# Value products of a pair of heads in two groups instead of five, in an attention and two-FFN kernel

## The chip, the cores and the metric

The kernel runs on one NeuronCore of a Trainium2 chip. The metric is device time in microseconds of one execution of the whole program, the median over several runs. Engines are named as in the profile: PE is TensorE (its weight loads, PEld, overlap its matmuls), DVE is VectorE, ACT is ScalarE, POOL is GpSimd, SP is SyncE.

## The reference

```
# q, k, v: (4 batches, 8 heads, 576 rows, 64 columns), float32; tau = 0.02
scores = matmul(q, k^T) / sqrt(64)
scores = where(scores >= max(scores) - tau, scores, -1e9)
attn   = exp(scores - max(scores));  attn = attn / (sum(attn) + 1e-9)
x      = matmul(attn, v), heads side by side      # 2304 tokens x 512
h      = x @ w_in;  g = max(h, 0) + alpha * min(h, 0);  x = g @ w_out       # 512 -> 2048 -> 512
h      = x @ w_in2; g = h * clip(h + 3, 0, 6) / 6;      out = g @ w_out2
```

## The kernel before

The work is cut into 16 pairs of heads (4 batches of 4 pairs) and into FFN passes. A pair has two heads with 576 query rows each. They are handled in nine score tiles (`NT = 9`): tiles 0 to 7 are four blocks of 128 queries, first head and second head in turn, and tile 8 holds the last 64 queries of both heads at once. Two tiles make a unit, the odd tile t of each couple ends it, and tile 8 is a unit of its own. So a pair has five units, which end at t = 1, 3, 5, 7 and 8, and cover 128, 128, 128, 128 and 64 queries of both heads.

For each tile, `do_S` forms the scores on PE (float32r) in PSUM, and `soft` takes the row maximum (DVE), the exponential (ACT) and the threshold with the row sum (DVE). At the end of a unit, `soft_norm` divides on POOL and DVE, `do_T` transposes the probabilities on PE, 128 columns at a time, and copies each bank of four transposes from PSUM to the tile `p` in SBUF with ACT (L427 for four blocks, L430 for the remaining one). `do_PV` then multiplies by the values.

A value product is an accumulation over five blocks of keys, for two heads. A value block is the 128x64 stationary operand, and the transposed probabilities of the unit are the moving operand: 128 queries, or 64 in the last unit. The first head writes partitions 0 to 63 of a PSUM tile of the pool `ps_ho`, the second head partitions 64 to 127. The operands are plain float32, and each such matmul appears in the trace as two load-and-multiply couples, so a group of one unit is 2 x 5 x 2 = 20 matmul rows on L444. ACT copies the group's result into `xo` (L450). After the last unit the pair's `xo` goes out: in the first batch it is split for the FFN's input, in later batches it is written to DRAM by two DMAs of SP.

`ps_ho` has two buffers. They are used in turn by the first FFN product `h` (L216, 12 matmuls of 512 columns), the second FFN product `o` (L245 in the first layer, L251 in the second, 12 matmuls of 512 columns for a tile), the value products `pv`, and, for the first pairs, transposes of inputs (L322). An `h` tile is read by ACT (`m`, L221 or L229) and then DVE (`g`, L223 or L231) before its buffer comes free; an `o` tile by ACT or DVE into `acc` (L504, L506, L508).

The attention of batch 0 runs first. From then on the FFN passes of the batch before are spread over the attention of the next one: after each score tile the main loop issues a proportional share of the FFN queue. Attention work is issued with a raised priority, and a planner orders the instructions of each engine before the program is built, by its own estimate of times. Within the first pass over each weight, weights that arrive as 64-bit numbers are decoded by ACT, DVE and POOL (L148 to L154) and written to a scratch in DRAM. The last FFN passes (the last batch, and all the 64-row remainders) run alone after the attention is over.

Of the kernel before, what the change touches and what calls it, by code (L numbers as in the profile page):

```python
# [9 lines left out]
F32 = mybir.dt.float32  # L10
# [9 lines left out]
P = 128  # L20
# [7 lines left out]
def f32(ap):  # L28
    return ap.bitcast(F32)
# [3 lines left out]
def kernel(  # L33
# [13 lines left out]
    nc = tc.nc  # L47
    B, H, S, D = q.shape
# [4 lines left out]
    SM = 512  # L53
    SR = S - SM
    SH = S // 2
    NP = H // 2
    NT = 9
    PB = NP * NT
    NB = S // P
# [11 lines left out]
    rem_blk = B  # L71

    dram = ctx.enter_context(tc.tile_pool(name="dram", bufs=1, space=DRAM))
    x1d = [dram.tile([ND, P, n], F32, name=f"x1d{i}") for i, n in enumerate(blocks)]

    def pool(stack, name, bufs, **kw):
        return stack.enter_context(tc.tile_pool(name=name, bufs=bufs, **kw))
# [22 lines left out]
    def split(hi, lo, src, lo_eng):  # L100
        nc.scalar.copy(hi, src)  # L101
        lo_eng.tensor_tensor(out=lo, in0=src, in1=f32(hi), op=ALU.subtract)  # L102
# [22 lines left out]
    for i in range(3 if wide else 0):  # L125
        t = const.tile([P, RA * RB, 2], U32, name=f"raw64{i}")
# [59 lines left out]
    def fetch(kind, c):  # L186
        if c < len(passes) * NF and (kind, c) not in ws:
            nm, ft, _, _, fresh = w_of(kind, c)
            w_fetch((kind, c), nm, ft, fresh)
# [71 lines left out]
    a3 = pool(att, "a3", 3, side="right")  # L261
    ps_s = pool(psum, "ps_s", 2, space=PSUM)
    ps_t = pool(psum, "ps_t", 2, space=PSUM)
    ps_ho = pool(psum, "ps_ho", 2, space=PSUM)
# [3 lines left out]
    for i in range(2):  # L268
        t = a1.tile([P, 2, P], F32R, tag=f"qr{i}", name=f"qr{i}")
# [5 lines left out]
    for i in range(2):  # L275
        t = a1.tile([P, 2, NB + 1, D], F32, tag=f"v{i}", name=f"v{i}")
# [9 lines left out]
    st = {}  # L286
# [61 lines left out]
    def prep(pi, t):  # L348
        if pi >= len(pairs):
            return  # L350
        if t == 0:
            prep_split(pi, "k")
        if t == 2:
            prep_load(pi, "v")
        if t in (1, 2, 3):
            prep_t(pi, "k", t - 1)
        if t == 3:
            prep_split(pi, "q")
            prep_load(pi + 1, "k")
        if t in (4, 5, 6):  # L360
            prep_t(pi, "q", t - 4)
        if t == 6:
            prep_load(pi + 1, "q")


    def do_S(i):
        pi, t = divmod(i, NT)
        s = st[pi]
        ps = ps_s.tile([P, 2, 512], F32, tag="s", name="s")
        if TILES[t] is None:  # L370
            mms = [(qr[pi % 2][:, h, :], h * W, a) for h in range(2) for a in range(2)]
        else:
            h, j = TILES[t]
            mms = [(s["q"][:, h * W + j * P:h * W + j * P + P], h * S, a) for a in range(2)]
        for half in range(2):
            for n, (w, c, a) in enumerate(mms):
                nc.tensor.matmul(ps[:, half, 0:SH], lhsT=w, rhs=s["k"][:, a, c + half * SH:c + half * SH + SH],  # L377
                                 start=(n == 0), stop=(n == len(mms) - 1))
        st[i, "s"] = ps
# [9 lines left out]
    def soft(i):  # L389
        h = 0 if TILES[i % NT] is None else TILES[i % NT][0]  # L390
        if h == 0:
            e = a3.tile([P, 2 * S], F32, tag="e", name="e", bufs=4)
            st["e"] = e, small("sm", 2, 3)
        e, sm = st["e"]
        ps = st.pop((i, "s"))[:, :, 0:SH]
        eh = v2(e[:, h * S:h * S + S])
        nmx, thr = small("nmx"), small("thr")
        nc.vector.tensor_reduce(out=nmx, in_=ps, axis=AX.XY, op=ALU.max, negate=True)  # L398
        nc.scalar.activation(eh, ps, AF.Exp, bias=nmx, scale=1.0)  # L399
        nc.vector.tensor_scalar(out=thr, in0=nmx, scalar1=-1.0, scalar2=ntau_sb, op0=ALU.mult, op1=ALU.add)  # L400
        nc.vector.scalar_tensor_tensor(out=eh, in0=ps, scalar=thr, in1=eh, op0=ALU.is_ge, op1=ALU.mult, accum_out=sm[:, h:h + 1])  # L401

    def soft_norm(n, tile_i):
        e, sm = st["e"]
        den, rc = small("den", 2), small("rc", 2, 3)
        nc.gpsimd.tensor_scalar(out=den[:, 0:n], in0=sm[:, 0:n], scalar1=1.0, scalar2=1e-9, op0=ALU.mult, op1=ALU.add)
        if wide and tile_i in EARLY:
            raw = raws[EARLY[tile_i]]
            nc.gpsimd.tensor_scalar(out=f32(raw[:, DM, :]), in0=den, scalar1=0.0, scalar2=0.0, op0=ALU.mult, op1=ALU.mult)
        nc.vector.reciprocal(rc[:, 0:n], den[:, 0:n])  # L410
        for h in range(n):
            eh = e[:, h * S:h * S + S]
            nc.gpsimd.tensor_scalar(out=eh, in0=eh, scalar1=rc[:, h:h + 1], scalar2=0.0, op0=ALU.mult, op1=ALU.add)  # L413
        if n == 1:
            nc.gpsimd.tensor_scalar(out=e[:, S:W], in0=e[:, SM:S], scalar1=1.0, scalar2=0.0, op0=ALU.mult, op1=ALU.add)

    def do_T(n):
        e, _ = st["e"]  # L420
        pt = a3.tile([P, 2 * NB + 1, P], F32, tag="p", name="p")
        for h in range(n):
            ps = ps_t.tile([P, NB, P], F32, tag="t", name="t")
            for kt in range(NB):
                c = h * W + kt * P
                nc.tensor.transpose(ps[:, kt], e[:, c:c + P], ident)  # L426
            nc.scalar.copy(pt[:, h * NB:h * NB + NB], ps)  # L427
        ps = ps_t.tile([P, SM], F32, tag="t", name="r")[:, 0:P]
        nc.tensor.transpose(ps, e[:, SM:W], ident)  # L429
        nc.scalar.copy(pt[:, 2 * NB], ps)  # L430
        return pt


    def do_PV(i, n, pt):
        pi, t = divmod(i, NT)
        b, hp = pairs[pi]
        vn = vs[pi % 2]
        m = P if n == 2 else SR
        pv = ps_ho.tile([P, SM], F32, tag="ho", name="pv")[:, 0:m]
        for kt in range(NB + 1):  # L440
            for h in range(2):
                blk = 2 * NB if kt == NB else kt + NB * h * (n - 1)
                c = SR * h * (2 - n)
                nc.tensor.matmul(pv[64 * h:64 * h + 64, :], lhsT=vn[:, h, kt, :], rhs=pt[:, blk, c:c + m],  # L444
                                 start=(kt == 0), stop=(kt == NB), skip_group_check=True)
        if "xo" not in st[pi]:
            st[pi]["xo"] = a2.tile([P, S], F32, tag="xo", name="xo")
        xo = st[pi]["xo"]
        j = t // 2
        nc.scalar.copy(xo[:, j * P:j * P + m], pv)  # L450
        if n == 1:
            if b == 0:
                split(x0[:, 0, hp], x0[:, 1, hp], xo[:, 0:SM], nc.gpsimd)
            else:
                nc.sync.dma_start(x1d[b][hp], xo[:, 0:SM])
            nc.sync.dma_start(x1d[rem_blk][hp, :, b * SR:(b + 1) * SR], xo[:, SM:S])
            del st[pi]

    box = {}
# [63 lines left out]
    def new_x():  # L526
        return xp.tile([P, 2, NKT, SM], F32R, tag="x", name="x")
# [16 lines left out]
    x0 = new_x()  # L544
# [25 lines left out]
    for i in range(NS):  # L570
        pi, t = divmod(i, NT)
        with tc.high_priority(offset=50):
            prep(pi + 1, t)
            do_S(i)
            soft(i)
        if t % 2 == 1 or t == NT - 1:
            with tc.high_priority(offset=50):
                n = 1 + t % 2
                soft_norm(n, i)
                do_PV(i, n, do_T(n))  # L580
            if i in EARLY:
                if len(ws) < 7:
                    ready(*EARLY[i])
                at = early.index(EARLY[i]) + 2
                if at < len(early):
                    fetch(*early[at])
        if i % PB == PB - 1:
            emitted.add(i // PB)
        while done < min(len(queue), (i + 1 - PB - LAG) * per):
            f, a = queue[done]  # L590
            f(*a)
            done += 1
# [16 lines left out]
    for layer in (1, 2):  # L609
# [6 lines left out]
        for m in range(len(seq) + LAGO):  # L616
            if m < len(seq):
                ft, blk = seq[m]
                n = blocks[blk]
                h = ps_h.tile([P, SM], F32, tag="h", name="h")  # L620
# [10 lines left out]
            ft, blk = seq[m - LAGO]  # L631
            gs = gss.pop(m - LAGO)
            n = blocks[blk]
# [3 lines left out]
            if layer == 1:  # L637
                for d in range(ND):
                    o = oa[d][:, 0:n] if blk < B else orr[d // 2][:, (d % 2) * 256:(d % 2) * 256 + n]
# [3 lines left out]
            else:  # L643
                for d in range((n + P - 1) // P):
                    o = oa[d] if blk < B else orr[d]
                    mm_o2(o, ws["o", c0 + ft], gs, d, n, first_, last_)
                    if last_:
                        t = ob.tile([P, SM], F32, tag="ob", name="ob")
# [38 lines left out]
```

## Time and profile before

| | |
|---|---|
| median of three runs | 1163.09 us (1161.37, 1163.09, 1163.73) |
| the profiled execution, its own time | 1161.51 us |
| its span in the profile | 1159.7 us |
| busy: PE, PEld, DVE, ACT, POOL | 1117.4, 927.7, 606.1, 697.6, 674.9 us |
| matmul rows, of them on L444 | 6944, of them 1600 |

The span is the time from the first to the last instruction of the profiled execution; 1.8 us of its own time lie around it. Busy times overlap across engines. A matmul's duration in the trace includes its passage through the array, so that consecutive matmuls overlap, and the distance from start to start tells more than the duration.

### The profile page before, as it was taken

To read this page: it belongs to the slowest core of one execution; us is meant where nothing else is said; L and a number is where in the kernel's file an instruction comes from. 1 tells how busy PE (TensorE), PEld (TensorE's weight loads), DVE (VectorE), ACT (ScalarE), POOL (GpSimd) and SP (SyncE) were. 2 spreads that over 40 slices of the span, in tenths; PEclk is the share of its full clock that TensorE was granted. 3 is DMA by queue.
4 is the path that set the end of the run, shared out by engine and by line. 5 is a ranking of instruction groups with operands and counts; after the bars stand their busy time and mean duration, and the time that the engine had idled before them with its cause. 6 is when DMAs were issued, how large, how long until landed. Compare 5 with 4: busy or idle time off the path is not lost.

```text
span 1159.7 us, 19517 instructions
## 1 busy us (share of the span) xinstructions
PE 1117.4 (96%) x6944; PEld 927.7 (80%) x6944; DVE 606.1 (52%) x1215; ACT 697.6 (60%) x1352; POOL 674.9 (58%) x726
## 2 busy tenths in 40 slices
PE   6998999999899999999999999999999999999998
PEld 5776888877778878787888888787878888888886
DVE  6889779898796616373454526273325222232221
ACT  6988888888877656465656555465435333344332
POOL 3777789998887755545456756544444343334432
PEclk9999999999999999999999999999999999999999
DMA  5546347765765432333324431322236222222211
GB/s 164 158 129 199 108 152 229 237 213 177 247 190 170 147 100 81 114 92 95 107 64 144 134 110 55 103 68 73 73 90 184 64 64 64 64 64 57 63 37 55
DMA packets 92770, 137.51 MB, mean 119 GB/s; under 512 B 19328, under 2 KB 48512, under 8 KB 92672
## 3 DMA queue, kind: packets, MB, share of 16 engines
q1 hardware_dynamic: 92672, 136.26, 39.7%
q8 instruction: 55, 0.90, 0.3%
q14 instruction: 43, 0.35, 0.1%
HBM read 101.72 MB, written 25.17 MB: 109 GB/s over the span
## 4 chain that ended last, share of the span: by engine, by line
PE 82%; ACT 7%; DVE 3%; DMA 3%; issue 2%; POOL 1%; SPq 0%; ACTq 0%; DVEq 0%; POOLq 0%
PE h L216 31%; PE o L245 14%; PE o L251 13%; PE s L377 6%; PE pv L444 6%; PE t L426 4%; PE r L251 2%; PE r L245 2%; PE pt L322 2%; ACT low L148 1%; ACT e L399 1%; ACT f L149 1%; PE r L429 1%; DMA wo<-f 1%; ACT p L427 1%
## 5 line engine op out<-in xcount | busy, mean ns | idle before, releaser
L216 PE MATMUL h<-x,wi 128*128 128x512 f32 (+1 forms) x1536 | 355.4, 380 | 1.4 <-DVE g L231 1.0
L216 PEld LDWEIGHTS h<-x,wi 128*128 128x128 f32 x1536 | 272.3, 188 | 54.3 <-ACT wi L101 1.2
L241 POOL TENSOR_TENSOR gs<-g,gs 128x512 fp32r<-128x512 f32 (+1 forms) x160 | 191.1, 1194 | 199.2 <-ACT gs L237 198.8
L251 PE MATMUL o<-wo,gs 128*128 128x512 f32 x768 | 194.1, 397 | 6.4 <-DVE g L231 4.2
L245 PE MATMUL o<-gs,wo 128*128 128x512 f32 x768 | 194.9, 397 | 3.7 <-DVE acc L506 1.4
L251 PEld LDWEIGHTS o<-wo,gs 128*128 128x128 f32 x768 | 140.2, 188 | 39.6 <-DVE g L231 6.5
L245 PEld LDWEIGHTS o<-gs,wo 128*128 128x128 f32 x768 | 140.2, 188 | 34.3 <-DVE acc L506 2.0
L223 DVE SCALAR_TENSOR_TENSOR g<-m,rest_sb,h 128x512 f32<-128x512 f32 x80 | 55.4, 693 | 174.8 <-ACT m L221 172.2
L231 DVE SCALAR_TENSOR_TENSOR g<-m,h 128x512 f32<-128x512 f32 x80 | 50.6, 632 | 164.4 <-ACT m L229 164.2
L102 POOL TENSOR_TENSOR wi<-st,wi 128x512 fp32r<-128x512 f32 x56 | 72.2, 1289 | 98.3 <-ACT wi L101 97.8
L401 DVE SCALAR_TENSOR_TENSOR e<-s,thr,e 128x576 f32<-128x576 f32 x144 | 116.0, 813 | 20.3 <-ACT e L399 17.8
L413 POOL TENSOR_SCALAR e<-e,rc 128x576 f32<-128x576 f32 x144 | 107.2, 755 | 26.7 <-DVE rc L410 22.5
L398 DVE TENSOR_REDUCE nmx<-s 128x1 f32<-128x576 f32 x144 | 107.6, 752 | 27.6 <-PE s L377 26.8
L229 ACT ACTIVATE m<-h,three 128x512 f32<-128x512 f32 x80 | 51.5, 645 | 116.5 <-PE h L216 116.5
L237 ACT CAST gs<-g 128x512 fp32r<-128x512 f32 (+1 forms) x160 | 93.2, 582 | 46.4 <-DVE g L231 15.1
L399 ACT ACTIVATE e<-s,nmx 128x576 f32<-128x576 f32 x144 | 106.8, 748 | 23.3 <-DVE nmx L398 22.1
L221 ACT ACTIVATE m<-h 128x512 f32<-128x512 f32 x80 | 44.5, 556 | 104.9 <-PE h L216 104.8
L444 PE MATMUL pv<-p,v 128*64 128x128 f32 (+1 forms) x1600 | 105.3, 268 | 1.9 <-ACT p L427 1.1
L377 PE MATMUL s<-ka,qt 128*128 128x288 f32 x512 | 100.8, 320 | 6.2 <-DVE thr L400 3.9
L444 PEld LDWEIGHTS pv<-p,v 128*64 128x64 f32 x1600 | 82.4, 137 | 23.0 <-issue 16.4
L102 POOL TENSOR_TENSOR wo<-st,wo 128x512 fp32r<-128x512 f32 x56 | 74.3, 1342 | 43.9 <-ACT wo L101 43.9
L101 ACT CAST wo<-st 128x512 fp32r<-128x512 f32 x96 | 57.1, 619 | 60.2 <-DMA st<-wo 52.0
(88 smaller groups left out, 1625.5 us busy)
## 6 DMA issues: line engine op xcount, KB each, us to landing
st<-wi SPq DMA_DIRECT2D x96, 256.0 KB, 2.6
st<-wo SPq DMA_DIRECT2D x96, 256.0 KB, 2.7
raw<-in_moe_w_in_dram SPq DMA_DIRECT2D x32, 512.0 KB, 4.3
raw<-in_moe_w_out_dram SPq DMA_DIRECT2D x32, 512.0 KB, 4.2
ka<-ka SPq DMA_DIRECT2D x30, 304.0 KB, 4.1
wi<-f SPq DMA_DIRECT2D x32, 256.0 KB, 4.0
wo<-f SPq DMA_DIRECT2D x32, 256.0 KB, 3.7
raw<-in_k_dram SPq DMA_DIRECT2D x16, 256.0 KB, 3.4
```

Of the source, the lines that this page charges most:

```text
L102: lo_eng.tensor_tensor(out=lo, in0=src, in1=f32(hi), op=ALU.subtract)
L216: nc.tensor.matmul(h[:, :n], lhsT=w[:, ws, kt * P:(kt + 1) * P], rhs=x[:, xs, kt, :n], start=(i == 0), stop=(i == len(steps) - 1))
L237: nc.scalar.copy(gs[:, 0, :n], g[:, :n])
L241: nc.gpsimd.tensor_tensor(out=gs[:, 1, :n], in0=g[:, :n], in1=f32(gs[:, 0, :n]), op=ALU.subtract)
L245: nc.tensor.matmul(o[:, :n], lhsT=w[:, ws, dt * P:(dt + 1) * P], rhs=gs[:, gsel, :n], start=fresh and start and i == 0, stop=stop and i == ...
L251: nc.tensor.matmul(o[:m, :], lhsT=gs[:, gsel, tt * P:tt * P + m], rhs=w[:, ws, :], start=start and i == 0, stop=stop and i == 2)
L377: nc.tensor.matmul(ps[:, half, 0:SH], lhsT=w, rhs=s["k"][:, a, c + half * SH:c + half * SH + SH], start=(n == 0), stop=(n == len(mms) - 1))
L398: nc.vector.tensor_reduce(out=nmx, in_=ps, axis=AX.XY, op=ALU.max, negate=True)
L399: nc.scalar.activation(eh, ps, AF.Exp, bias=nmx, scale=1.0)
L401: nc.vector.scalar_tensor_tensor(out=eh, in0=ps, scalar=thr, in1=eh, op0=ALU.is_ge, op1=ALU.mult, accum_out=sm[:, h:h + 1])
L413: nc.gpsimd.tensor_scalar(out=eh, in0=eh, scalar1=rc[:, h:h + 1], scalar2=0.0, op0=ALU.mult, op1=ALU.add)
L444: nc.tensor.matmul(pv[64 * h:64 * h + 64, :], lhsT=vn[:, h, kt, :], rhs=pt[:, blk, c:c + m], start=(kt == 0), stop=(kt == NB), skip_group_ ...
```

## The change

From the second batch on, nothing is multiplied at the ends of units t = 1 and t = 5. At t = 3 one group takes the units of t = 1 and t = 3 together, with 256 queries as one moving operand of two runs of 128. At t = 8 one group takes the units of t = 5 and t = 7 in the same way (256 queries), then the last unit's 64 queries into the columns behind them, so that one PSUM tile holds 320 columns. ACT's copy into `xo` follows the group: 256 and 320 columns in place of four of 128 and one of 64. In the first batch the value products stay five groups.

The tile `p` becomes two tiles that hold two units each (`p`, two buffers), and one for the last unit (`p1`, one buffer), in place of three tiles of one unit. The transposes and their copies write the same blocks into the new places.

```
-    def do_T(n):
+    def do_T(n, t):
         e, _ = st["e"]
-        pt = a3.tile([P, 2 * NB + 1, P], F32, tag="p", name="p")
+        if n == 1:
+            pt = a3.tile([P, 1, NB + 1, P], F32, tag="p1", name="p1", bufs=1)
+        elif t % 4 == 1:
+            pt = a3.tile([P, 2, 2 * NB + 1, P], F32, tag="p", name="p", bufs=2)
+        else:
+            pt = st["p"][0]
+        dst = pt[:, t % 4 // 2 if n == 2 else 0]
...
-            nc.scalar.copy(pt[:, h * NB:h * NB + NB], ps)
+            nc.scalar.copy(dst[:, h * NB:h * NB + NB], ps)
...
-        nc.scalar.copy(pt[:, 2 * NB], ps)
-        return pt
+        nc.scalar.copy(dst[:, n * NB], ps)
+        st["p"] = st.get("p", []) * (t % 4 != 1) + [pt] * (n == 1 or t % 4 == 1)

-    def do_PV(i, n, pt):
+    def do_PV(i):
...
-        m = P if n == 2 else SR
-        pv = ps_ho.tile([P, SM], F32, tag="ho", name="pv")[:, 0:m]
-        for kt in range(NB + 1):
-            for h in range(2):
-                blk = 2 * NB if kt == NB else kt + NB * h * (n - 1)
-                c = SR * h * (2 - n)
-                nc.tensor.matmul(pv[64 * h:64 * h + 64, :], lhsT=vn[:, h, kt, :], rhs=pt[:, blk, c:c + m],
-                                 start=(kt == 0), stop=(kt == NB), skip_group_check=True)
+        if b == 0:
+            parts = [(1, st["p"][1], 0)] if t == NT - 1 else [(2, st["p"][0], t % 4 // 2)]
+        elif t in (3, NT - 1):
+            parts = [(2, st["p"][0], None)] + [(1, p1, 0) for p1 in st["p"][1:]]
+        else:
+            return
+        pv = ps_ho.tile([P, SM], F32, tag="ho", name="pv")
+        at = 0
+        for n, pt, u in parts:
+            m = SR if n == 1 else P if u is not None else 2 * P
+            for kt in range(NB + 1):
+                for h in range(2):
+                    blk = n * NB if kt == NB else kt + NB * h * (n - 1)
+                    o = pv[64 * h:64 * h + 64, at:at + m]
+                    if n == 1:
+                        r = pt[:, 0, blk, SR * h:SR * h + m]
+                    elif u is None:
+                        o, r = o.rearrange("p (u q) -> p u q", u=2), pt[:, :, blk, :]
+                    else:
+                        r = pt[:, u, blk, :]
+                    nc.tensor.matmul(o, lhsT=vn[:, h, kt, :], rhs=r, start=(kt == 0 and at == 0), stop=(kt == NB), skip_group_check=True)
+            at += m
...
-        j = t // 2
-        nc.scalar.copy(xo[:, j * P:j * P + m], pv)
-        if n == 1:
...
+        end = S if t == NT - 1 else t // 2 * P + P
+        nc.scalar.copy(xo[:, end - at:end], pv[:, 0:at])
+        if t < NT - 1:
+            return
...
                 soft_norm(n, i)
-                do_PV(i, n, do_T(n))
+                do_T(n, t)
+                do_PV(i)
```

## Rows read from the trace of the kernel before

**Rows 1.** The page: PE's line of busy times, and the granted clock in 40 slices.
```profile
PE 1117.4 (96%) x6944; PEld 927.7 (80%) x6944; DVE 606.1 (52%) x1215; ACT 697.6 (60%) x1352; POOL 674.9 (58%) x726
...
PEclk9999999999999999999999999999999999999999
```
**Rows 2.** Three stretches: from:to, length, busy time by engine, clock, DMA.
```profile
117.00:200.00 83.00, 82.66 (x549) 69.47 (x549) 65.18 (x135) 69.20 (x135) 67.95 (x75) 1.00 0.55 167
200.00:350.00 150.00, 140.83 (x867) 114.69 (x866) 129.49 (x250) 124.75 (x231) 130.24 (x131) 1.00 0.68 209
350.00:865.00 515.00, 507.30 (x3156) 417.12 (x3155) 240.61 (x473) 291.97 (x569) 285.55 (x296) 1.00 0.35 102
```
**Rows 3.** The chain that ended last, same stretches in the same order, shares by line.
```profile
by line: PE h L216 34.0%; PE o L245 26.7%; PE s L377 13.1%; PE pv L444 10.5%; PE t L426 9.3%; PE pt L322 4.0%; PE r L429 1.4%; ACT e L399 0.8%; ACT p L427 0.6%; PE pt L325 0.4%; issue 0.1%
...
by line: PE h L216 17.6%; PE o L245 7.8%; PE o L251 6.9%; issue 6.4%; DMA wo<-f 5.3%; ACT f L149 4.8%; ACT low L148 4.2%; PE s L377 4.2%; DMA wi<-f 3.8%; ACT e L399 3.1%; ACT gs L237 2.4%; PE pv L444 2.1%; DMA raw<-in_moe_w_out_dram 2.1%; A
...
by line: PE h L216 34.1%; PE o L251 17.8%; PE o L245 17.6%; PE s L377 7.2%; PE pv L444 7.2%; PE t L426 5.9%; PE pt L322 1.6%; issue 1.6%; PE r L429 1.0%; ACT m L229 0.8%; ACT wi L101 0.7%; DVE g L231 0.7%; DMA st<-wo 0.5%; DVE acc L508 0.4%
```
**Rows 4.** The tile pv alone, same stretches: busy PE, PEld, ACT, with counts.
```profile
117.00:200.00 83.00, 9.69 (x140) 7.37 (x140) 1.90 (x7) 1.00 0.55 167
200.00:350.00 150.00, 13.42 (x220) 10.97 (x220) 2.84 (x11) 1.00 0.68 209
350.00:865.00 515.00, 50.53 (x840) 41.32 (x840) 10.55 (x42) 1.00 0.35 102
```
**Rows 5.** The timeline of PE around two value groups: start, length, what.
```profile
424.08 1.31 PE L444 MATMUL pv<-p,v 128*64 128x128 f32 x20
425.33 3.01 PE L245 MATMUL o<-gs,wo 128*128 128x512 f32 x12
428.27 0.80 PE L444 MATMUL pv<-p,v 128*64 128x64 f32 x20
429.00 0.33 PE L429 MATMUL r<-ident,e 128*128 128x128 f32 x1
```
**Rows 6.** The timeline of PE cut to one couple before each group's edge.
```profile
427.95 0.39 PE L245 MATMUL o<-gs,wo 128*128 128x512 f32 x1
...
425.12 0.28 PE L444 MATMUL pv<-p,v 128*64 128x128 f32 x2
```
**Rows 7.** Groups by line and shape: count, busy us, mean ns, idle before.
```profile
L444 PE MATMUL pv<-p,v 128*64 128x128 f32 x1280 | 91.5, 279 | 0.8 <-DVE g L231 0.8
...
L444 PEld LDWEIGHTS pv<-p,v 128*64 128x64 f32 x1600 | 82.4, 137 | 23.0 <-issue 16.4 <-ACT p L427 1.4 <-DVE g L231 1.0
L427 ACT COPY p<-t 128x512 f32<-128x512 f32 x144 | 82.3, 596 | 11.6 <-PE t L426 11.5
...
L450 ACT COPY xo<-pv 128x128 f32<-128x128 f32 x64 | 17.1, 267 | 6.8 <-PE pv L444 6.2
...
L444 PE MATMUL pv<-p,v 128*64 128x64 f32 x320 | 13.8, 227 | 1.1 <-ACT p L427 1.1
...
L450 ACT COPY xo<-pv 128x64 f32<-128x64 f32 x16 | 3.5, 216 | 15.7 <-PE pv L444 15.6
```
**Rows 8.** PE's waits from 350 to 865: in total, times, longest.
```profile
PE o L251 <- DVE g L231: 2.2, 6, 0.4
...
PE o L245 <- DVE g L223: 0.6, 2, 0.3
```
**Rows 9.** The timeline around one such wait, PE and DVE.
```profile
408.83 1.31 PE L444 MATMUL pv<-p,v 128*64 128x128 f32 x20
410.43 0.50 PE L245 MATMUL o<-gs,wo 128*128 128x512 f32 x1 [0.29 <-DVE g L223]
...
409.63 0.75 DVE L223 SCALAR_TENSOR_TENSOR g<-m,rest_sb,h 128x512 f32<-128x512 f32 x1 [1.72 <-ACT m L221]
```
**Rows 10.** PE's waits from 200 to 350: in total, times, longest.
```profile
PE o L251 <- DVE g L231: 2.0, 3, 1.2
...
PE o L245 <- ACT xo L450: 1.4, 1, 1.4
```

More of the change, by code (lines that the diff above doesn't have):

```diff
@@ L448, in do_PV @@
         xo = st[pi]["xo"]
-        j = t // 2
-        nc.scalar.copy(xo[:, j * P:j * P + m], pv)
-        if n == 1:
[L452 to L457, printed above, removed]
+        end = S if t == NT - 1 else t // 2 * P + P
+        nc.scalar.copy(xo[:, end - at:end], pv[:, 0:at])
+        if t < NT - 1:
+            return
+        if b == 0:
+            split(x0[:, 0, hp], x0[:, 1, hp], xo[:, 0:SM], nc.gpsimd)
+        else:
+            nc.sync.dma_start(x1d[b][hp], xo[:, 0:SM])
+        nc.sync.dma_start(x1d[rem_blk][hp, :, b * SR:(b + 1) * SR], xo[:, SM:S])
+        del st[pi]
     box = {}
```

## The prediction

> **What bounds the kernel now.** I read the page first. PE is busy 96% of the span, no other engine above 60%, and its granted clock is full in every slice [rows 1], the 2.4 GHz level, so the clock plays no part. An average of that kind hides stages, so I next cut out the time in which batches 1 to 3 do their attention, 117 to 865 us, in three stretches [rows 2]. From 117 to 200 PE is busy all but 0.3 us, from 350 to 865 all but 7.7 of 515. In between, from 200 to 350, PE lacks 9.2 us of 150 and DVE, ACT and POOL are each busy 125 to 130: there the weights are decoded beside the attention. The chain of waits says the same [rows 3]: in the first and third stretch nearly all of it is PE's lines, and L444 holds 10.5% and 7.2%. In the middle one the PE lines add up to about 39%, the rest passes between ACT, DMA and issue. After 865 no value product runs. So an instant of PE saved from 117 to 200 or from 350 to 865 shortens the program, and one saved from 200 to 350 only in part.
>
> The value products of the twelve changed pairs are 140 + 220 + 840 = 1200 rows on L444 [rows 4], 100 to a pair: 1.4 pairs in the first stretch, 2.2 in the second, 8.4 in the third.
>
> **What a group costs on PE.** A group of 128 queries has 20 rows. They last 1.31 us together and one lasts 0.279 [rows 5, 7], so starts are (1.31 - 0.279) / 19 = 0.054 us apart. The two heads run side by side on the two halves of the array, so I count couples: 0.109 us each, ten of them 1.09. For 64 queries it is (0.80 - 0.227) / 19 = 0.030, a couple 0.060, ten 0.60.
>
> A group costs more than its couples. From its first start to the next group's start are 1.25 us, and 0.73 for 64 queries [rows 5]. On the way in, the 512-column matmul ahead of the group starts 0.32 us before it [rows 6, 5], where such matmuls otherwise stand (3.01 - 0.39) / 11 = 0.24 apart [rows 5, 6]: 0.08 more. On the way out, the last couple starts 0.21 us ahead of the next group where couples stand 0.109 apart. So a group of 128 costs 1.25 + 0.08 = 1.33 us, of which 0.24 are its edges; one of 64 costs 0.81, of which 0.21 are edges.
>
> **The change, part by part.** *Wider matmuls.* No row has a plain float32 moving operand of 256 columns. If it costs what two of 128 do, a couple takes 0.218 us; the straight line through 0.060 and 0.109 gives 0.207. I take 0.216, near the upper end, since 128 columns are the nearer row, and keep both. Ten couples are 2.16 (2.07 to 2.18) and a group 2.40 with its edges.
>
> *Fewer groups.* A pair costs 4 x 1.33 + 0.81 = 6.13 us before. After, it costs 2.40 at t = 3 and 2.40 + 0.60 = 3.00 at t = 8, where the 64 queries follow with no edge between: 5.40. That saves 0.73 a pair, nearly all of it edges of the three groups that go (0.69). In the two PE-bound stretches it is 9.8 x 0.73 = 7.2 us. In the middle, 2.2 x 0.73 = 1.6 are saved on PE, and I take the 39% that PE holds of the chain: 0.6 (0 to 1.6).
>
> *Waits behind short groups.* `h`, `o` and `pv` share two PSUM buffers, so behind `h` and `pv` an `o` needs the buffer of that `h`. At 408.83 a value group begins after `h`; DVE reads that `h` until 410.38 and `o` starts at 410.43, after a wait of 0.29 [rows 9]. The reader needs 1.55 us from the end of `h`, longer than a group of 1.33 and shorter than one of 2.40. Where no value group stands any more, `o` takes the other buffer. Either way the wait goes. From 350 to 865 there are 2.2 + 0.6 = 2.8 us of it, eight times [rows 8]. I take all (0 to 2.8). From 200 to 350 waits of the kind are 2.0 and 1.4 us [rows 10]; I take none (0 to 3.4), as other engines set the pace there.
>
> *ACT's copies.* Before, 4 x 267 + 216 = 1284 ns a pair. No row copies 256 or 320 columns; between 267 ns for 128 and 596 for 512 [rows 7] a line gives 377 and 431, so 0.48 us less a pair, 5.7 in all. ACT is busy 292 of 515 us in the long stretch, and PE's work hides the copies; I count nothing. In the middle stretch 2.2 x 0.48 = 1.0 us at most.
>
> *New waits.* The group at t = 3 waits for the same copies of `p` as the unit of t = 3 did. At t = 8 the 64-query part waits for the last unit's copies on L427 (and a 128-column one, which a copy of that size on L450 puts at 0.27): 0.6 + 0.27 us, hidden under the 2.16 of the 256-query part ahead of it in PE's queue. Without that cover it would be 0.9 a pair. The products of t = 1 and t = 5 are later by two and three score tiles; nobody reads `xo` before t = 8, and the DMAs of SP are issued there as before, with the same bytes.
>
> *The tiles.* The transposes and their copies are as many and as large. A `p` tile is written again six or more tiles after its last reader: with twelve pairs in 748 us [rows 2] a tile is 6.9 us, so the cover is over 40 us, and the cost nothing. The first batch keeps its five groups and its order.
>
> *The sum.* 7.2 + 0.6 + 2.8 = 10.6 us. The profiled execution took 1161.5, so 1150.9; the median of the runs lies 1.6 above it, which gives 1152.5, and I write 1152. Bounds of the costs: at the small end, edges in the PE-bound stretches alone and couples of 0.218, 9.8 x 0.69 = 6.8; at the large end 12 x 0.73, the flat line (12 x 20 x 0.009 = 2.2), both kinds of waits (2.8 + 3.4) and ACT's 1.0: 18.2. That is 1145 to 1156.
>
> **A page against the rows.** A couple of 128 stands 0.109 us apart, and one of 64, with stationary operands of the same size (all 1600 loads are 128x64 [rows 7]), 0.060. So the loads are not what sets 0.109, and wider operands buy no cheaper columns. The Trainium skill, TensorE: Matmul & The Clock Gate, Part 2, step 3, says that throughput is purely one column a cycle, which would make 128 columns 0.053 us at 2.4 GHz and leave about half of 0.109 to something else that merging halves. The trace does not agree with that for these float32 operands, as the 0.049 us between the two rows for 64 further columns shows.
>
> **Rivals.** *The loads were the bound after all.* Then a couple of 256 would cost 0.109 and each of the two merged groups in a pair save another 1.07 us: 12 x 2.14 = 26 more, 1127. The 0.060 couple speaks against it.
>
> *The edges go, but half of the gain comes back.* The planner orders all queues anew, and a PE with fewer edges meets other waits: the same stretch has waits of PE on DVE and ACT that now last tenths. Half of 10.6 leaves 1158. For it speaks that PE has 7.7 us idle in 515 already; against it, that FFN work fills PE at any time and the others are half idle.
>
> *No change.* The pace is set elsewhere, say by the share of FFN work that the main loop lets out for each score tile. Then fewer edges become idle time: 1162 to 1164. The long stretch, with PE at 98.5%, speaks against it.
>
> *Slower: the long group holds up the softmax.* PE works in order, so a score matmul or transposes queued behind a merged group come 2.40 - 1.33 = 1.07 us later at t = 3 and 3.00 - 0.81 = 2.19 at t = 8: 3.26 a pair, 39 us over twelve. Where the attention's chain is the path, that is lost. It is partly so from 200 to 350, where ACT's exponential and the scores stand in the chain [rows 3]: 2.2 x 3.26 = 7.2 there. The break-even is 10.6 of 39, 27%; at 40%, 15.6 - 10.6 = 5 us slower, 1168. Against it: the earlier units' groups no longer stand in that queue, and other engines have over 200 us to spare in the long stretch.
>
> **Numbers.** The forecast 0.62, loads 0.03, half of it 0.13, no change 0.10, slower 0.12. What a measurement of this kernel can tell from no change is about 0.2%, 2.3 us. So faster 0.78, same 0.10, slower 0.12. The range goes from 1146, near the large end, up over the case of half the gain to 1162: it leaves out the loads, the slower case and some of no change, about 0.2. The forecast's own range is 1146 to 1157.
>
> **What would show it.** L444 should have 400 + 720 = 1120 rows, in batches 1 to 3 with 480 of 256 columns and 240 of 64; twenty of 256 should last about 0.108 x 19 + 0.35 = 2.4 us. The stretch that was 350 to 865 should be shorter by some 9 us, the first by 1, the middle by 1 or less, and the time up to 117 and after 865 unchanged. The waits of `o` on DVE `g` should be gone there. I am wrong if a couple of 256 columns differs much from 0.216, if the long stretch has as much more idle PE as it has fewer edges, or if the middle grows.

## The result and the profile after

The changed kernel takes 1145.32 us (median, 1144.27 to 1146.52), the kernel before 1163.09. The ratio is 0.985, with a 95% interval from 0.984 to 0.987: 17.3 us faster. The forecast was 1152, 10.6 us faster, and 1145.3 lies just under its range. The prediction's sum had its large end at 18.2 us, 1145; the range that it wrote began at 1146. So the direction was right and the gain some 60% larger than forecast.

The profiled execution after took 1145.86 us, with a span of 1144.1; that is 15.7 us less than the profiled one of before, and the accounts below are of these two. It is less than 17.3 because the profiled execution of before was 1.6 us faster than its median. The page after, PE's line and the granted clock:

```profile
PE 1109.8 (97%) x6464; PEld 913.9 (80%) x6464; DVE 611.9 (53%) x1215; ACT 692.4 (61%) x1316; POOL 681.5 (60%) x726
...
PEclk9999999999999999999999999999999999999999
```

Against [rows 1], PE is busy 7.6 us less, and the rest of the span, in which PE does nothing, fell from 42.3 to 34.3, by 8.0. The forecast had 7.8 us of work (8.8 saved on PE, of which it let 7.8 count) and 2.8 of waits. So the work came out nearly as foretold, and the idle time fell by almost three times as much.

The value products after, by line and shape:

```profile
L464 PE MATMUL pv<-p,v 128*64 128x256 f32 x480 | 57.7, 384 | 0.3 <-DVE acc L525 0.3
...
L464 PE MATMUL pv<-p,v 128*64 128x128 f32 x320 | 28.1, 285 | 0.0
...
L464 PE MATMUL pv<-p,v 128*64 128x64 f32 x320 | 13.2, 223 | 1.1 <-ACT p L433 1.1
...
L470 ACT COPY xo<-pv 128x320 f32<-128x320 f32 x12 | 5.3, 439 | 5.3 <-PE pv L464 5.3
...
L470 ACT COPY xo<-pv 128x256 f32<-128x256 f32 x12 | 4.4, 368 | 3.8 <-PE pv L464 3.8
```

The counts are as foretold, 480 + 240 rows in batches 1 to 3. ACT's copies cost 439 and 368 ns, where a line through two rows gave 431 and 377. PE's timeline around one group at t = 8:

```profile
422.30 0.95 PE L377 MATMUL s<-ka,qt 128*128 128x288 f32 x6
423.18 2.96 PE L464 MATMUL pv<-p,v 128*64 128x256 f32 x40
426.07 3.02 PE L245 MATMUL o<-gs,wo 128*128 128x512 f32 x12
```

All 40 rows, 256 and then 64 columns, stand in one piece. From its first start to the start of `o` are 2.89 us. With 0.09 for the way in that is 2.98, where the forecast had 3.00. So the price of a group was right, that of the wider operand with it.

Where the time went is seen by cutting both traces at the same work: the starts of the 1st, 385th and 1153rd matmul row on L216. Windows before (from:to, length, busy PE, PEld, DVE, ACT, POOL, clock, DMA):

```profile
122.60:394.90 272.30, 262.74 (x1656) 216.47 (x1654) 218.79 (x429) 218.06 (x411) 228.37 (x233) 1.00 0.63 193
394.90:872.60 477.70, 470.40 (x2903) 386.89 (x2902) 215.94 (x425) 267.62 (x522) 255.91 (x265) 1.00 0.33 95
```

The same after:

```profile
122.50:392.70 270.20, 264.36 (x1518) 215.15 (x1517) 225.04 (x439) 220.71 (x403) 232.10 (x240) 0.99 0.63 196
392.70:857.10 464.40, 460.67 (x2581) 373.96 (x2580) 215.56 (x414) 259.81 (x494) 259.92 (x261) 1.00 0.34 97
```

Ahead of and behind these windows the two kernels differ by 0.1 us each. The first of the two is 2.1 us shorter, the second 13.3. But the first also holds more work: without value products (418 rows of it before, 258 after) it has 1260 rows where it had 1238. These 22 rows of scores and transposes last about 0.12 us each from start to start, an estimate of 2.7 us. At equal work the first window gains 4.8 us and the second 10.6; the forecast had 2.1 and 8.4 for them. PE's idle time falls from 9.6 to 5.8 in the first and from 7.3 to 3.7 in the second.

### The profile page after: what moved, and what is told of

Same layout as the page of the kernel before. It is cut to its first block, busy times and chain, and to the rows that moved or that the text cites. A ratio compares the mean times of both kernels' runs of the same rounds, so it can differ in the third digit from the quotient of the medians.

```text
span 1144.1 us, 18508 instructions
## 1 busy us (share of the span) xinstructions
PE 1109.8 (97%) x6464; PEld 913.9 (80%) x6464; DVE 611.9 (53%) x1215; ACT 692.4 (61%) x1316; POOL 681.5 (60%) x726
## 4 chain that ended last, share of the span: by engine, by line
PE 81%; DVE 5%; ACT 4%; issue 4%; POOL 3%; DMA 2%; SPq 0%; DVEq 0%; ACTq 0%; POOLq 0%
PE h L216 32%; PE o L245 14%; PE o L251 13%; PE pv L464 7%; PE s L377 6%; PE t L432 4%; PE r L251 2%; PE r L245 2%; PE pt L322 1%; DVE nmx L398 1%; DVE e L401 1%; DMA st<-wo 1%; POOL nat L102 1%; DVE low L150 1%; POOL gs L241 1%
## 5 line engine op out<-in xcount | busy, mean ns | idle before, releaser
L216 PE MATMUL h<-x,wi 128*128 128x512 f32 (+1 forms) x1536 | 356.8, 381 | 0.0
L216 PEld LDWEIGHTS h<-x,wi 128*128 128x128 f32 x1536 | 271.9, 188 | 54.7 <-issue 1.2
L413 POOL TENSOR_SCALAR e<-e,rc 128x576 f32<-128x576 f32 x144 | 112.5, 792 | 27.7 <-DVE rc L410 26.1
L464 PE MATMUL pv<-p,v 128*64 128x256 f32 (+2 forms) x1120 | 97.0, 310 | 1.4 <-ACT p L433 1.1
L433 ACT COPY p<-t 128x512 f32<-128x512 f32 x144 | 82.1, 594 | 23.4 <-PE t L432 14.4
```

What stands on the lines that cost most here:

```text
L216: nc.tensor.matmul(h[:, :n], lhsT=w[:, ws, kt * P:(kt + 1) * P], rhs=x[:, xs, kt, :n], start=(i == 0), stop=(i == len(steps) - 1))
L464: nc.tensor.matmul(o, lhsT=vn[:, h, kt, :], rhs=r, start=(kt == 0 and at == 0), stop=(kt == NB), skip_group_check=True)
```

## The experiments

All were timed beside the kernel before, 4 to 12 executions each. Times faster or slower are ratio minus one, times 1163 us.

Theory A: the gain is the edges of the groups that go and the waits behind short groups. Theory B: wider operands are cheaper by the column. Theory C: the new order of the planner brought the surplus by luck. A piece or unbroken group is a run of value rows on PE with nothing between them. The ring is the two PSUM buffers in which `h`, `o` and `pv` turn.

**Five groups with the new tiles.** In the changed kernel:

```
-        if b == 0:
+        if True:
             parts = [(1, st["p"][1], 0)] if t == NT - 1 else [(2, st["p"][0], t % 4 // 2)]
```

> The changed kernel with its new tiles p and p1, but five value groups in every pair, as before: the tiles alone. Theory A (what is gained are the edges of the groups that go, 0.24 us each, and the waits of o behind short groups) and theory B (wider operands are cheaper) both expect the time of before within 1 us. Theory C (a good part of the gain is that the planner came to another order by chance) allows any shift, say 2 to 5 us to either side.

Measured: 1167.31 us, ratio 1.0032 (1.0019 to 1.0044), 3.7 us slower. So the tiles bring nothing; if anything they cost. Theories A and B, which expected no shift beyond 1 us, missed here; theory C allows one of this size.

**The same bursts with narrow operands.**

```
-            parts = [(2, st["p"][0], None)] + [...]
+            parts = [(2, st["p"][0], 0), (2, st["p"][0], 1)] + [...]
```

> The same two bursts and two PSUM tiles a pair as after the change, but each 256-query operand cut into two accumulations of 128 queries: 40 couples of 128 in place of 20 of 256. Theory A: couples of 0.109 in place of 0.216 cost 12 x 20 x 0.002 = 0.5 us, so 0 to 2 us slower than the changed kernel, 16 to 18 faster than before. Theory B: the widening is what pays, so most of the gain goes, and it is at most 9 us faster than before.

Measured: 1150.11 us, ratio 0.9894 (0.9881 to 0.9908), 12.3 us faster. Theory B falls: twice the matmuls keep most of the gain. But 5 us less than the changed kernel is more than theory A's 0 to 2. PE's busy time is 1108.8 us and its idle time 39.2, where the changed kernel has 1109.8 and 34.3, so the loss is idle time.

**A PSUM tile for each unit**, inside the bursts:

```
+        for n, pt, u in parts:
+            pv = ps_ho.tile([P, SM], F32, tag="ho", name="pv")
...
+            nc.scalar.copy(xo[:, at:at + m], pv[:, 0:m])
+            at += m
```

> The bursts at the ends of the units t = 3 and t = 8 are kept, but each unit is multiplied on its own: a PSUM tile of its own, 128 or 64 columns, its own copy to xo. Theory A, by edges: the value rows stand in 78 unbroken groups on PE in place of 65 after the change and 103 before, 13 x 0.24 = 3.1 us, so 14 to 15 us faster than before. If the two PSUM buffers are what counts (five tiles a pair turn in the ring again), the waits of o on DVE g and on the copies to xo come back and it is 6 to 10 us faster than before.

Measured: 1154.31 us, ratio 0.9929 (0.9917 to 0.9941), 8.3 us faster. By its time this is the case in which the two PSUM buffers count. The trace does not bear that out. Its windows, and under them those of the narrow bursts, which have two PSUM tiles a pair in place of five:

```profile
123.50:397.70 274.20, 264.87 (x1679) 219.73 (x1679) 221.58 (x438) 221.37 (x415) 230.89 (x238) 1.00 0.63 193
397.70:864.50 466.80, 462.12 (x2880) 385.60 (x2880) 216.13 (x414) 262.02 (x518) 260.34 (x261) 1.00 0.35 97
...
117.10:394.20 277.10, 267.79 (x1721) 223.79 (x1720) 226.01 (x447) 224.57 (x411) 234.25 (x242) 1.00 0.63 192
394.20:861.00 466.80, 461.19 (x2881) 385.86 (x2880) 213.73 (x414) 258.83 (x494) 259.42 (x261) 1.00 0.35 97
```

PE is idle 9.3 us in the first window of both, and 4.7 in the second where the narrow bursts have 5.6. The 4 us between the two kernels are busy PE, 1113.5 against 1108.8 us, with 78 pieces against 68; more tiles in the ring brought no more idle time.

**Three groups**, at t = 3, 7 and 8:

```
-        elif t in (3, NT - 1):
-            parts = [(2, st["p"][0], None)] + [(1, p1, 0) for p1 in st["p"][1:]]
+        elif t in (3, NT - 2, NT - 1):
+            parts = [(2, st["p"][0], None)] if t < NT - 1 else [(1, st["p"][1], 0)]
```

> 256 queries at t = 3, 256 at t = 7, 64 at t = 8: one group more a pair than after the change, 77 unbroken groups in place of 65. Theory A: 12 x 0.21 = 2.5 us slower than the changed kernel, 15 faster than before. Theory C expects no relation to the number of groups.

Measured: 1156.63 us, ratio 0.9949 (0.9937 to 0.9962), 5.9 us faster. A miss: 11 us behind the changed kernel where 2.5 were expected. Busy PE is 2.4 us above the changed kernel's, as expected; the rest is idle time, 42.6 us, as much as before the change.

**One part of the batches at a time**, by `if b != 1:` and `if b < 2:` in place of `if b == 0:`.

> The change in batch 1 alone, whose attention runs from about 117 to 370 us, so over the whole stretch in which weights are decoded; batches 2 and 3 keep five groups. The recorded forecast gives this part 1.0 us in the first stretch, 0.6 in the middle and 0.3 behind it: 2 us faster than before. If PE's time counts in the middle stretch too, 4 x 0.73 = 2.9 us of edges and up to 3.4 us of waits behind value groups: 5 to 7 us faster.

Measured: 1163.82 us, ratio 0.9999 (0.9989 to 1.0010): no change, where 2 or 5 to 7 us were expected.

> The change in batches 2 and 3 alone. The recorded forecast gives this part 8 x 0.73 + 2.8 = 8.6 us. If the middle stretch earned nothing beyond the forecast, this holds nearly all of the 17.8 us that the change brought: 15 or more. If edges and waits count alike everywhere, 8 to 10.

Measured: 1152.53 us, ratio 0.9898 (0.9883 to 0.9913), 11.9 us faster, between its two expectations. Taken by their totals the two look as if batch 1 gained nothing. The windows, cut at the same rows of L216, say otherwise. Batch 1 alone:

```profile
122.50:392.50 270.00, 264.61 (x1539) 216.00 (x1538) 225.89 (x441) 221.24 (x404) 233.10 (x240) 0.99 0.62 195
392.50:876.00 483.50, 469.39 (x2881) 384.90 (x2880) 212.90 (x412) 263.17 (x517) 258.31 (x259) 1.00 0.33 94
```

Five groups with the new tiles, which is the same kernel without batch 1's merging:

```profile
123.50:398.30 274.80, 265.31 (x1678) 219.41 (x1677) 225.69 (x440) 221.48 (x415) 231.81 (x239) 1.00 0.61 190
398.30:877.80 479.50, 469.42 (x2880) 384.69 (x2879) 214.81 (x411) 262.71 (x517) 259.21 (x260) 1.00 0.33 96
```

Batches 2 and 3 alone, first window:

```profile
123.50:399.20 275.70, 265.52 (x1658) 218.66 (x1657) 225.74 (x440) 221.32 (x414) 231.55 (x239) 1.00 0.62 192
```

Merging batch 1 brings the 385th row 5.8 us forward (398.3 to 392.5), and 6.5 in the pair of the changed kernel and batches 2 and 3 alone (399.2 to 392.7). The recorded forecast for it was 2. In the window PE's idle time falls by 4.1 and 4.3 us of this, its busy time by 0.7 and 1.2. In the first pair 4.0 us were given back in the long window, where five groups a pair cost 14.1 us of idle PE with batch 1 merged and 10.1 without, 7.3 in the kernel before, against 3.7 after the change. Against its own counterpart each kernel with batch 1 merged is faster in its total too, by 3.8 and 5.5 us. What sets how much five groups lose there is not shown. It is not how far the attention is ahead of the FFN: in the kernels with 14.1 and 10.1 the same 1738 rows without value products start before the 385th row.

**Value products out of the ring.** In the kernel before, the PSUM tile of a group comes from the pool of the transposes:

```
-        pv = ps_ho.tile([P, SM], F32, tag="ho", name="pv")[:, 0:m]
+        pv = ps_t.tile([P, SM], F32, tag="t", name="pv")[:, 0:m]
```

> The kernel before, with one edit: the value products' PSUM tiles come from the pool of the transposes, so that they no longer turn in the ring of h and o. The waits of o behind short groups go (some 6 us in all). The planner breaks the value rows into more pieces, 136 unbroken groups in place of 103, 33 x 0.24 = 7.9 us of edges. Theory A: 0 to 4 us slower than before. If the waits alone make the gain and edges cost nothing: 5 to 7 us faster. Waits of transposes on the shared pool may add to either.

Measured: 1160.5 us, ratio 0.9972 (0.9961 to 0.9983), 3.3 us faster, between the two expectations: both effects are there, and the idle time fell by more than the 6 us that theory A took. Its long window:

```profile
386.70:871.90 485.20, 484.25 (x2959) 393.95 (x2958) 225.15 (x451) 274.55 (x539) 263.80 (x275) 1.00 0.32 95
```

and PE's line of its page:

```profile
PE 1126.1 (97%) x6944; PEld 924.8 (80%) x6944; DVE 606.7 (52%) x1215; ACT 696.9 (60%) x1352; POOL 675.7 (58%) x726
```

Idle PE in the long window fell to 0.9 us, as it should if the waits there were the ring's. But the edit also put PE's work in another order: only a third of the places in PE's order hold the same kind of row as before. Busy PE grew by 8.7 us with 33 more pieces, 0.26 us each, for the same matmuls.

**The first batch too**, by `if False:` in place of `if b == 0:`.

> The change in the first batch as well, where no FFN work runs beside the attention: 16 groups of 128 and 64 fewer edges there, 56 unbroken groups in place of 65. PE is idle 19 us in that stretch and the chain goes through the softmax, so edges there should be nearly free: 0 to 2 us faster than the changed kernel. If the later products hold up the first batch's end, up to 3 us slower than it.

Measured: 1157.74 us, ratio 0.9950 (0.9938 to 0.9963), 5.8 us faster, 11.5 behind the changed kernel: a miss, at most 3 were expected. PE's waits ahead of the first FFN row:

```profile
PE t L432 <- POOL e L413: 7.8, 7, 1.9
```

That row is absent after the change. Transposes wait for probabilities that POOL has not yet scaled, and the first FFN row comes at 133.7 us in place of 122.5. Over that stretch the mean granted clock is 0.92, where the kernel after the change has 0.99:

```profile
0.00:133.70 133.70, 107.77 (x718) 78.41 (x718) 98.78 (x241) 102.41 (x197) 80.17 (x128) 0.92 0.50 144
```

Behind it, its windows of 271.1 and 464.2 us are within 1 us of the changed kernel's.

**The planner's order.** To tell luck from cause, the raise of priority was set to 45 and 55 in both kernels, which changes the planner's order and no work:

```
-        with tc.high_priority(offset=50):
+        with tc.high_priority(offset=45):
```

> The kernel before with the raise of priority of the attention's instructions at 45 in place of 50: the same work and value groups (104 unbroken ones in place of 103), in another order of the planner's. Theory A (edges and waits of the groups) expects before within 1 us. Theory C (the order by itself moves the waits by some us) expects 2 to 5 us to either side, with PE's busy time unchanged within 1 us and all of it in PE's idle time.

Measured: ratio 0.9995 (0.9986 to 1.0003).

> As the run at 45, with the raise at 55: 103 unbroken groups. Theory A: within 1 us of before. Theory C: 2 to 5 us to either side, in PE's idle time.

Measured: ratio 0.9990 (0.9981 to 0.9999).

> The changed kernel with the raise at 45: 65 unbroken groups, as at 50. Theory A: 17 to 18 us faster than before, like the changed kernel. Theory C: the edges (9 us) and the waits of o behind short groups (3 us) stay, what lies above is luck of one order: 9 to 14 us faster than before.

Measured: 1146.63 us, ratio 0.9851 (0.9837 to 0.9864).

> As the run before, with the raise at 55. Theory A: 17 to 18 us faster than before. Theory C: 9 to 14 us faster.

Measured: 1145.04 us, ratio 0.9838 (0.9824 to 0.9851). The gain is 17 to 19 us in three orders, and the kernel before moves by 1. That speaks against theory C, but not with much force, for the three orders are near one another: by the traces 92 to 95% of the places in PE's order hold the same kind of row as at 50. In five groups with the new tiles it is 55% of those of the kernel before, and that kernel took 3.7 us more. A shift by the order of some 4 us is not ruled out.

**Out of the ring, in few pieces.** Theory R (the ring of two PSUM buffers) and theory S (the softmax's order) were left. The edit of the pool above, and one more raise of priority around `do_PV`, in the kernel before and in the changed one (shown in the latter):

```
+                with tc.high_priority(offset=400):
+                    do_PV(i)
```

> The kernel before with the value products' PSUM tiles in the pool of the transposes, and their matmuls raised in priority once more, so that they stand in fewer pieces than in pv_in_t: 120 unbroken groups. If the two-buffer ring of h, o and pv makes the waits that the change took away (theory R), PE's idle time between the starts of the 4th and 12th 96-row portion of L216 falls from 7 to about 1 us, and the kernel is 16 x 0.24 = 4 us faster than pv_in_t by edges: 7 us faster than before. If those waits come from elsewhere (theory S, the softmax's order), the idle time there stays at 5 us or more.

Measured: 1160.85 us, ratio 0.9977 (0.9966 to 0.9988), 2.7 us faster. Its long window:

```profile
387.40:875.10 487.70, 485.83 (x2983) 392.73 (x2982) 226.60 (x451) 275.10 (x538) 263.96 (x276) 1.00 0.34 95
```

and PE's line of its page:

```profile
PE 1126.1 (97%) x6944; PEld 926.6 (80%) x6944; DVE 609.7 (52%) x1215; ACT 698.8 (60%) x1352; POOL 677.3 (58%) x726
```

The idle time of 1.9 us there is theory R's, not theory S's. The 4 us by edges did not come: with 16 pieces fewer, the time and busy PE are those of the first run with the value products out of the ring. The mean granted clock of this execution was 0.993, which may hide them; the executions at 0.998 took 1158.0 to 1159.3 us.

> The changed kernel with the same two edits: pv out of the ring, 58 unbroken groups. Theory R: with the ring's waits gone on both sides, the merging is worth its edges alone, (120 - 58) x 0.24 = 15 us between this run and five_out_of_ring, in PE's busy time, and about 3 to 6 us less than the changed kernel, so 20 to 23 us faster than before. Theory S: as the changed kernel, 17 us, or less where the transposes now wait for a long group's tile.

Measured: 1137.26 us, ratio 0.9785 (0.9772 to 0.9797), 25 us faster than before and 8 than the changed kernel; it is the fastest of all. Its long window:

```profile
388.10:848.40 460.30, 458.23 (x2544) 371.19 (x2543) 212.64 (x419) 259.46 (x490) 258.55 (x263) 1.00 0.34 98
```

and PE's line of its page:

```profile
PE 1099.1 (97%) x6464; PEld 906.0 (80%) x6464; DVE 603.7 (53%) x1215; ACT 690.5 (61%) x1316; POOL 680.8 (60%) x726
```

Idle PE in the long window is 1.9 us with five groups and 2.1 with two: without the ring, merging has no waits left to take away there, as theory R says. The gap between the two kernels is then 22 to 24 us in time and 27 in busy PE (1126.1 against 1099.1), and by pieces it should have been 15; the gain of 25 us also lies above theory R's 20 to 23. Up to half of the excess in busy PE may be the clock: the mean granted clock was 0.993 in the run of five groups and 1.000 in the other. The rest was not found.

Nor are the 8 us to the changed kernel a matter of waits. Over the whole span PE is idle 36.3 us here and 34.3 in the changed kernel; busy PE is 10.7 us less, of which seven fewer pieces explain about 2 and the clock up to 3.4. Up to the 385th row on L216 PE is idle 28.1 us, 24.4 in the changed kernel and 28.8 before: where weights are decoded, taking `pv` out of the ring brought little, for other waits took the place of the ring's. The largest from the first FFN row to the 385th:

```profile
PE pv L464 <- ACT p L433: 5.7, 8, 1.4
```


**One group of 512**, with one tile `p` for four units:

```
-        elif t in (3, NT - 1):
+        elif t == NT - 1:
...
+                        o, r = o.rearrange("p (u q) -> p u q", u=4), pt[:, :, blk, :]
```

> One group a pair at t = 8, with 512 queries as one operand of four runs, and 64 queries behind it in a PSUM tile of their own; there is one tile p for four units. 58 unbroken groups in place of 65: 1.7 us of edges less than the changed kernel. The transposes of the next pair's first unit wait for the group to read p, and the group is 4.6 us long at t = 8: if that holds nothing up, 18 to 20 us faster than before; if the softmax or the transposes wait, up to 10 us slower than the changed kernel.

Measured: 1159.25 us, ratio 0.9964 (0.9952 to 0.9976), only 4.2 us faster, which is slower than both of its expectations. PE is idle 15.3 us in its first window and 6.8 in its second:

```profile
114.40:395.90 281.50, 266.18 (x1425) 208.85 (x1422) 221.77 (x431) 221.85 (x405) 231.51 (x238) 0.99 0.60 188
395.90:869.40 473.50, 466.70 (x2484) 369.32 (x2483) 227.76 (x441) 264.95 (x505) 266.29 (x269) 1.00 0.35 97
```

So the gain doesn't go on with the length of the group. This kernel changed the group and the number of tiles `p` at once, and which of the two costs was not separated.

## Why the prediction was right or wrong

*The price of a group: right.* 2.98 us measured for the long group, 3.00 forecast, with a couple of 256 columns at 0.216 as taken.

*The edges: right in size, as far as shown.* They can be checked by dose. Five kernels had the full clock until their last microseconds, and differ in the number of pieces in which the value rows stand. Besides the kernel before with 103 pieces and 1117.4 us of busy PE [rows 1] and the one with 136 and 1126.1, and that of the merged groups out of the ring, with 58 and 1099.1, these are three groups, with 77 pieces:

```profile
PE 1112.2 (96%) x6464; PEld 909.3 (79%) x6464; DVE 611.5 (53%) x1215; ACT 693.6 (60%) x1328; POOL 682.8 (59%) x726
```

and the narrow bursts, with 68:

```profile
PE 1108.8 (97%) x6944; PEld 930.4 (81%) x6944; DVE 607.3 (53%) x1215; ACT 691.2 (60%) x1316; POOL 681.1 (59%) x726
```

From 136 to 68 pieces busy PE falls by 17.3 us, 0.25 a piece, where the forecast read 0.24 and 0.21 off two groups. It does so although the narrow bursts have 480 matmul rows more than three groups. From one kernel to the next it is 0.26, 0.20 and 0.38 a piece, and the kernel with 58 lies 7 us below this line. So the pieces are not all that moves busy PE between these kernels; what else does is open. The Trainium skill, TensorEngine Tiling (Array Packing), Key Properties, says that changing the tiling mode drains TensorE; value products use the array in two halves of columns and their neighbours do not, and the price of an edge here agrees with that; no run here separates the mode from the type of the operands.

*The rival of the loads: rightly low.* The couple of 256 takes 0.216 and not 0.109, and cutting the operand in two cost 5 us of 17, in idle time.

*The middle stretch: wrong, and the larger miss.* This is the step that failed: from 200 to 350 us the prediction had 2.0 and 1.4 us of waits and wrote "I take none (0 to 3.4), as other engines set the pace there". Merging batch 1 brought the 385th row of L216 forward by 5.8 and 6.5 us where the forecast gave it 2, and over 4 us of each are idle PE. In the window from the 1st to the 385th row, waits of `o`, `h` and `pv` for a reader of the ring (on `g`, `acc` and `xo`) were 6.0 us before: the 3.4 of [rows 10], 0.6 more of `o`, and

```profile
PE h L216 <- DVE g L231: 1.0, 1, 1.0
PE pv L444 <- DVE g L231: 0.8, 1, 0.8
...
PE h L216 <- ACT xo L450: 0.2, 1, 0.2
```

After the change they are 2.3:

```profile
PE o L251 <- DVE g L231: 1.2, 2, 0.9
...
PE o L251 <- DVE acc L527: 0.5, 1, 0.5
...
PE o L245 <- DVE g L223: 0.3, 1, 0.3
PE pv L464 <- DVE acc L525: 0.3, 1, 0.3
```

That other engines set the pace there was too strong: PE was still busy 94% of the stretch [rows 2]. The other step for this stretch, "I take the 39% that PE holds of the chain", can be off by 1.0 us at most, the part of its 1.6 that the forecast left out.

*The waits in the long stretch: right in kind, somewhat short in size.* The forecast took all 2.8 us of `o` behind a value group [rows 8], and none of these eight waits is left. But idle PE fell by 3.6 us in this window, and busy PE by some 7.0 at equal work, where the 7.6 pairs in it should save 5.5. PE's waits for the ring after, in this window:

```profile
PE o L251 <- DVE g L231: 1.5, 3, 1.0
PE o L251 <- DVE acc L527: 0.8, 1, 0.8
```

Before, it had 2.8 us more in four waits of `o` for `acc`, which I had not counted:

```profile
PE o L245 <- DVE acc L506: 1.4, 2, 0.7
PE o L251 <- DVE acc L508: 1.4, 2, 0.8
```

One of them in PE's timeline:

```profile
473.25 2.83 PE L245 MATMUL o<-gs,wo 128*128 128x512 f32 x11
475.92 2.88 PE L216 MATMUL h<-x,wi 128*128 128x512 f32 x12
...
478.87 0.46 PE L245 MATMUL o<-gs,wo 128*128 128x512 f32 x1
...
480.12 2.10 PE L245 MATMUL o<-gs,wo 128*128 128x512 f32 x8 [0.72 <-DVE acc L506]
```

Here the new `o` waits for the reader of the `o` that has just ended, while `h` holds the other buffer; no value group stands between, in none of the four. What is left after the change has no value group between either. So the ring makes these waits, but short groups do not, and that three of the four are gone comes with the new order. All ring waits of this window, 5.6 us, became 2.3; with the 3.7 of the window ahead these are 7.0 of the 8.0 us of idle PE that went.

That short groups in the ring were the cause is shown in part. For it speak the eight waits, each behind a value group, and the long window of the runs with `pv` out of the ring: 0.9, 1.9 and 2.1 us idle, whatever the number of groups. Against it stands that these edits changed the order as well, that they left the idle time up to the 385th row at 25.5, 28.0 and 28.1 us where it was 28.8 before and 24.4 after, and that five tiles a pair in the ring, in the run with a tile for each unit, had no more idle time than two in the narrow bursts.

*The tiles: put at nothing.* With five groups they came with 3.7 us more; whether they cost anything under merged groups no run separates.

*The slower rival: not seen where it was placed.* In batches 1 to 3 no such loss shows; the 385th row came earlier. Where no FFN work stands beside the attention, in the first batch, merging brought the first FFN row 11 us later, though part of that is the clock. That PE's order behind a long group is what delays the softmax there was not traced.

*Still open.* Idle PE in the decoding window was 9.3 in the narrow bursts and in the run with own tiles, 12.0 with three groups, and 5.8, 7.9 and 7.3 in the changed kernel at three priorities. Why narrow bursts, with the same PSUM tiles as the changed kernel, keep 1.4 to 3.5 us more of it is not settled. Nor is why three groups lose 11 us, with idle time as before the change at three tiles a pair. So how much of the 8 us of idle time is owed to the ring, and how much to the order that came with the new groups, stays open.

## What to carry to other kernels

Read the price of a switch on PE from the starts on both sides of a group and multiply it by the pieces in the order that is built, not by the groups in the source; here it was about 0.25 us a piece over four kernels, and 0.20 to 0.38 from one to the next. Where several kinds of tiles turn in a ring of two PSUM buffers, list every wait for a reader of that ring, in every stretch where PE is nearly full, and look at what stands between before calling a short tile its cause. Taking the short tiles out of the ring and merging them brought 25 us where merging alone brought 17, but the difference was busy PE and not waits. In this kernel a merged group paid where other work was at hand for PE: the same edit in the stretch without FFN work cost 11 us.

## What the runs showed of the hardware

The granted clock fell for a few microseconds in the changed kernel, which was not foreseen. Windows of the kernel after, around one such place:

```profile
275.00:280.00 5.00, 2.66 (x15) 1.99 (x14) 4.98 (x13) 5.00 (x10) 4.83 (x7) 1.00 0.79 236
280.00:285.00 5.00, 5.00 (x23) 4.42 (x22) 4.05 (x8) 3.90 (x8) 4.83 (x8) 0.66 0.67 244
```

PE had been busy 2.66 of 5 us, and in the next 5 the mean granted clock was 0.66: for 3.4 us it stood at the level of 1.2 GHz, then again at 2.4. Apart from the last microseconds it happened twice in this execution, here and at 106 us, and not in that of before. The change need not be the cause of the earlier one: the kernel before had one at 114 and at 106 us with the raise of priority at 45 and 55. Busy PE fell by 7.6 us; without these two it might have fallen by up to 3.4 us more, an estimate from half the rate over twice 3.4 us. Here a pause of PE was followed by work at half the rate, so it can have cost more than its own length.
